# Two queues for the first load, and an earlier place for the first ordinary pair's q and k, in a linear-attention and feed-forward kernel

## The chip, the cores and the metric

The kernel runs on one core of one Trainium2 chip. The metric is the device time of one execution in microseconds (us), less is better; a time of several runs is their median. The engines are TensorE (PE, matmuls; its weight loads are a row of their own, PEld), VectorE (DVE), ScalarE (ACT), GpSimd (POOL) and SyncE (SP). They run side by side and wait for each other by semaphores. SP, ACT and POOL each issue DMA transfers into a queue of their own; 16 DMA engines move the data of all queues.

## The reference

Two layers, one after the other. The first is linear attention with decay over blocks of 64 tokens, for 4 batches, 8 heads, 768 tokens and a head size of 64:

```python
for b in range(nb):                                   # nb = 768 / 64 = 12
    sl = slice(b * block, (b + 1) * block)
    qb, kb, vb = q[:, :, sl], k[:, :, sl], v[:, :, sl]
    intra = np.einsum('bhic,bhjc->bhij', qb, kb) * Dmask[None]      # lam^(i-j), j <= i
    intra = np.einsum('bhij,bhjd->bhid', intra, vb)
    inter = np.einsum('bhid,bhde->bhie', qb * lam_pow[None], kv_state)
    out[:, :, sl] = intra + inter
    kb_dec = kb * rev_pow[None]
    kv_state = lam_block[None, :, None, None] * kv_state + np.einsum('bhsd,bhse->bhde', kb_dec, vb)
```

The second is a gated feed-forward layer on the 3072 tokens, with a model size of 512 and a hidden size of 2048:

```python
x = attn_out.transpose(0, 2, 1, 3).reshape(3072, 512)
h = x @ w_in                                          # 512 x 2048
g = h * np.cos(h)
out = g @ w_out                                       # 2048 x 512
```

All inputs and the output are float32; the kernel multiplies in bfloat16 and sums in float32.

## The kernel before

**Tiling.** Tokens are cut into 24 groups of 128. The feed-forward layer takes them in tiles of 4, 2, 2, 2, 2, 2, 2, 4 and 4 groups (`TILES`). For a tile, 16 hidden slices are made (`hidden`, L732, into `ps_h`), ACT takes the cosine (L738), DVE multiplies (L744, into `g`), and the second product (`project`, L778, into `ps_f`) sums the 16 slices in four steps of four, each step with one quarter of w_out. ACT copies the sum out (L792) and SP stores it.

**Attention.** The first four groups are two *spans*: the first 256 tokens of batch 0 and of batch 1, two neighbouring tokens in a partition. A span's q, k and v come in one load each (`add_span_load`, L259, issued at L253). DVE or POOL scales q and k by powers of lam (`prep`, L593), TensorE transposes them (L601, `ps_t`), ACT copies the transposes out (L604), then follow scores (L612), masking on DVE (L617), values (L638), the carried state (L625, L644) and the copies into `xT` (L652), which the first feed-forward tile reads. All other groups go in *ordinary pairs*, group n of two batches. Their loads are `add_load` (L275); a pair's q is scaled on DVE and POOL (L329), its k converted on ACT or POOL (L333), its v scaled (L337). The first ordinary pair consists of groups 4 and 5. Its q and k are transposed on TensorE (L359) and copied by DVE (L362); later pairs are transposed by DMA (L365).

**Order.** No scheduler of the compiler decides the order. The kernel lists all work as tasks with an engine, a planned duration, dependencies and a priority; `Planner.order` simulates the engines with these numbers and writes the instructions in the order of planned start. `SETUP` holds the times at which the planner takes each engine, and the DMA engines, to be free at first. Its numbers are not the chip's; they only set the order. Each engine then runs its own instructions strictly in that order, so a waiting instruction holds everything behind it on its engine.

**Loads.** The string `ORDER` names the early loads in order: q0, k0, q1, k1, v0, v1 are the spans'; i0 to i5 the six parts of w_in (of 2, 2, 1, 3, 4, 4 hidden slices); o0 to o3 the quarters of w_out; q4, q5, k4, k5 the first ordinary pair's; v4 and v5 follow. The spans' q and k and all ordinary loads are issued by SP, the spans' v and all weights by POOL, which converts float32 to bfloat16 on the way. `start` (L252) can make an issue wait for another load to have landed: v0 waits for q0 (the argument `kept[0:1]`); q4 waits for a gate product of the first feed-forward tile (`pace`, L755, three slices before its last); o3 waits for q4; v4 waits for k4. In the program before, POOL issues v0, v1, i0, i1, prepares k of span 1, issues i2, i3, i4, i5, o0, o1, o2, then o3. SP issues q0, k0, q1, k1 of the spans, then q4, q5, k4, k5, v4, v5. When TensorE has made the first tile's 16 slices, it runs seven steps of `ps_f` (with o0, o1 and o2), the eight transposes of q of the first ordinary pair, two more steps, the transposes of k, and so on.

**The very first microseconds.** ACT loads lam (L188) and an activation table (L189); TensorE spreads lam over all partitions (`ps_lam`, L875) between filler matmuls that keep it busy (`keep_awake`, L861, `ps_idle`); ACT and DVE make the scales from it (L877 to L891), ACT loads the table of the sine (L893).

Of the kernel before, what the change touches and what calls it, by code (L numbers as in the profile page):

```python
# [10 lines left out]
F32 = mybir.dt.float32  # L11
# [7 lines left out]
SPANS = 2  # L19
# [15 lines left out]
STATE_OUT = [("ACT", "ACT"), ("ACT", "ACT")]  # L35
ORDER = "q0 k0 q1 k1 v0 v1 i0 i1 i2 i3 i4 i5 o0 o1 o2 q4 q5 k4 k5 o3"

# [19 lines left out]
class Planner:  # L57
# [3 lines left out]

    SETUP = {"POOL": 3.7, "DVE": 4.4, "ACT": 6.0, "SP": 0.85, "DMA": 1.95}

# [81 lines left out]
def kernel(  # L145
# [41 lines left out]
    lam_row = consts.tile([1, H], F32)  # L187
    nc.scalar.dma_start(out=lam_row, in_=lam.unsqueeze(0))  # L188
    nc.scalar.preload_act_table_set("natural_log_exp_and_others")  # L189
    ones = consts.tile([1, P], F32)  # L190
# [40 lines left out]
    halves = [slice(i * D, (i + 1) * D) for i in range(2)]  # L231
    live = {}

# [24 lines left out]

    def add_span_load(name, src, x, prio, deps):  # L259
        def emit(_):  # L260
            if on_pool:
                t = span_v[x]
            else:
                if ("raw", x) not in live:
                    live["raw", x] = work.tile([P, 2, H, 2, D], F32, tag="g", name="sp_f")
                t = live[name, "sp", x] = live["raw", x][:, "qk".index(name[0])]
            return start(nc.gpsimd if on_pool else nc.sync, t.rearrange("u h s d -> u h (s d)"),
                         src[x, :, 0:2 * P, :].rearrange("h (u s) d -> u h (s d)", s=2), deps)

        on_pool = name == "v_f"  # L270
        issue, load_t[name, "sp", x] = dma("POOL" if on_pool else "SP", 1.5, 1.0 if on_pool else 0.5, emit, prio, deps,
                                           lat=0.95 if on_pool else 1.0)
        return load_t[name, "sp", x]

    def add_load(n, name, src, prio, deps=()):  # L275
        b, c = where(n)

        def emit(_):
            t = loads.tile([P, H, D], F32, tag=name, name=name)
            live[name, n] = t  # L280
            i = start(nc.sync, t, src[b, :, c * P:(c + 1) * P, :].transpose([1, 0, 2]), deps)
            if (name, n) == ("q_f", 2 * SPANS):

                tc.add_manual_dep(i.ins, pace[0].ins.ins.name, mybir.DependencyInfo(
                    mybir.DependencyClass.Sync, mybir.DependencyReason.DATA), reason="order of loads")
            return i

        issue_t[name, n], load_t[name, n] = dma("SP", LOAD_US, 0.85, emit, prio, deps, get=name,
                                                lat=1.9 if name == "v_f" and n < 2 * SPANS + 2 else 1.0)
        return load_t[name, n]  # L290
# [3 lines left out]
    def add_w(which, c, prio, deps=()):  # L294
        def emit(_):
            if which == "in":
# [7 lines left out]
        _, w_t[which, c] = dma("POOL", 2.68 * part, 0.8, emit, -2000.0 if early else prio, deps,  # L304
                               lat=1.2)
        return w_t[which, c]
# [272 lines left out]
    def add_span(x):  # L579
# [75 lines left out]
        s_first = None  # L655
        so, kt, v_t = [[], []], [], [load_t["v_f", "sp", x]]
        for hp in range(2):
            eq, ek = QK[x]["q"][hp], QK[x]["k"][hp]
            a = pl.add(eq, us[eq], [load_t["q_f", "sp", x]], partial(prep, name="q", hp=hp, e=eq), pa(-0.9 + 0.1 * hp))
            kt.append(pl.add(ek, us[ek], [load_t["k_f", "sp", x]], partial(prep, name="k", hp=hp, e=ek), pa(-0.9 + 0.1 * hp)))  # L660
            if x:
# [50 lines left out]

    h_last, o_last = {}, {}
    hid, closing = [], None

    def add_ffn(i):
# [4 lines left out]
        for f in range(KF):  # L721
            gate[f] = []
            blocks = [(0, 2), (2, 4)] if i == 0 and f < SPLIT else [(0, nb)]
            for b0, b1 in blocks:
# [27 lines left out]
                a.frees = [d]  # L752
                gate[f].append(d)
                if i == 0 and f == KF - 3:
                    pace.append(d)  # L755
# [61 lines left out]
    for at, name in enumerate(names):  # L817
# [3 lines left out]
        if name == f"q{2 * SPANS}":  # L821
            deps = []
        if name == f"v{2 * SPANS}":
            deps = [load_t["k_f", 2 * SPANS]]
        if name == "o3":
            deps = [load_t["q_f", 2 * SPANS]]
# [13 lines left out]
    add_span_state(first_scores, prio_attn(2 * SPANS, 0.2))  # L840
    pr = SPANS
    for i in range(len(TILES)):
        while 2 * pr < first[i + 1]:
            if pr + 1 in ALONE:
                add_scores(pr + 1, prio_attn(2 * pr + 2, 0.2))
# [26 lines left out]

    keep_awake(1.2, 1.6)
    lam_ps = bank((idle.bank[0] + 4) % BANKS, [P, H], F32, "ps_lam")
# [18 lines left out]
    nc.scalar.activation(warm, halfpi, AF.Sin)  # L893
    now = 2.8
    for t in plan:
        if t.eng == "PE" and t.start < lead_end.start + 1e-6:
            keep_awake((t.start - now) * 0.95 if now < 3.0 else t.start - now, now)
            now = t.end
        if t.emit:
            t.ins = t.emit(t)  # L900
# [30 lines left out]
```

## Time and profile before

| what | us |
|---|---|
| median of 3 runs | 203.09 (202.97 to 203.18) |
| the profiled execution, whole | 202.54 |
| its span on the core | 200.8 |
| TensorE busy in it | 195.9 |
| `ps_h` L732, 596 matmuls, and `ps_f` L778, 400 matmuls, busy | 91.1 and 91.4 |
| DVE, ACT, POOL busy | 116.3, 119.4, 64.9 |
| bytes moved by DMA | 33.93 MB, 169 GB/s on average |

The profile is one execution, taken by the hardware profiler. All times in it are microseconds from the span's start. A line of the timeline has the start, the duration, the engine, the source line, the operation, output and inputs, and in brackets the engine's idle time before it and what ended that. Lines with a q behind an engine's name (SPq, ACTq) are DMA issues; their duration is that of the issue, not of the transfer. The chain of waits goes back from the last instruction, at each step to what released it, and is shown in order of time with start and duration. In lists of DMA queues, q1 is SP's queue, q10 ACT's and q0 POOL's, and the numbers are packets, MB and the time that packets took as a share of the 16 engines' time.

### The profile page before, as it was taken

How to read it: one execution, taken by the hardware profiler on the slowest of the kernel's cores; microseconds unless marked ns; L12 is line 12 of the kernel's file. 1: busy time of each engine (PE TensorE's matmuls, PEld its weight loads, DVE VectorE, ACT ScalarE, POOL GpSimd, SP SyncE). 2: the span in 40 equal slices, each digit the busy share in tenths (PEclk: the TensorE clock that was granted, in tenths of full speed). 3: DMA queues.
4: the chain of work that ended last, by engine and by line, in shares of the span. 5: the costliest groups of instructions: out<-in, count | busy, mean ns of one | idle time of the engine just before them, and what ended most of it. 6: DMA issues, size and time to landing. Idle time of an engine off the chain costs nothing.

```text
span 200.8 us, 5951 instructions
## 1 busy us (share of the span) xinstructions
PE 195.9 (98%) x2473; PEld 116.8 (58%) x2473; DVE 116.3 (58%) x230; ACT 119.4 (59%) x241; POOL 64.9 (32%) x85
## 2 busy tenths in 40 slices
PE   6999999999999999999999999999999999999994
PEld 3477444558757757766658676755445544444452
DVE  3978771269756948758458575835588354444001
ACT  4878771149658768666639666644887564345120
POOL 5893003085235360635555353545500000000000
PEclk9999999999999999999999999999999999999999
DMA  5999999999889997999999899979910010111112
GB/s 163 303 190 204 203 199 216 209 238 225 200 197 225 262 202 177 239 179 253 189 275 245 188 207 194 277 141 261 243 23 3 3 52 0 52 55 52 52 52 104
DMA packets 96620, 33.93 MB, mean 169 GB/s; under 512 B 84690, under 2 KB 93650, under 8 KB 96594
## 3 DMA queue, kind: packets, MB, share of 16 engines
q1 hardware_dynamic: 89088, 28.78, 63.2%
q0 software_dynamic: 7360, 4.72, 16.4%
q8 instruction: 19, 0.31, 0.7%
q10 hardware_dynamic: 146, 0.07, 0.1%
q14 instruction: 7, 0.06, 0.1%
HBM read 27.26 MB, written 6.29 MB: 167 GB/s over the span
## 4 chain that ended last, share of the span: by engine, by line
PE 95%; DMA 2%; ACT 0%; DVE 0%; SPq 0%; issue 0%; ACTq 0%; DVEq 0%
PE ps_h L732 42%; PE ps_f L778 42%; DMA sp_f<-in_k_dram 2%; PE ps_s L407 2%; PE ps_o L502 2%; PE ps_o L470 2%; PE ps_kv L419 1%; PE ps_t L601 1%; PE ps_s L612 1%; PE ps_o L638 1%; PE ps_kv L625 1%; PE ps_x L470 0%; PE ps_idle L870 0%; PE ps_t L359 0%; DVE k_sp L593 0%; PE ps_o L644 0%
## 5 line engine op out<-in xcount | busy, mean ns | idle before, releaser
L744 DVE TENSOR_TENSOR g<-ps_h,cos 128x256 bf16<-128x256 f32 (+1 forms) x149 | 73.1, 501 | 42.0 <-ACT cos L738 41.1
L738 ACT ACTIVATE cos<-ps_h,halfpi 128x256 f32<-128x256 f32 (+1 forms) x149 | 75.9, 536 | 29.3 <-PE ps_h L732 28.2
L778 PE MATMUL ps_f<-w_out_sb,g 128*128 128x512 bf16 (+2 forms) x400 | 91.4, 371 | 0.0
L732 PE MATMUL ps_h<-xT,w_in_sb 128*128 128x256 bf16 (+1 forms) x596 | 91.1, 303 | 0.0
L732 PEld LDWEIGHTS <-w_in_sb 128*128 128x128 bf16 x596 | 57.5, 98 | 30.1 <-DVE xT L510 0.4
L778 PEld LDWEIGHTS <-g 128*128 128x128 bf16 x400 | 37.6, 98 | 37.2
L329 POOL TENSOR_TENSOR qk<-q_f,q_scale 128x512 bf16<-128x512 f32 x19 | 20.0, 1067 | 34.7 <-DMA q_f<-in_q_dram 17.6
L792 ACT COPY o_sb<-ps_f 128x512 f32<-128x512 f32 (+1 forms) x24 | 13.7, 572 | 24.7 <-PE ps_f L778 24.5
L337 POOL TENSOR_TENSOR v_s<-v_f,v_scale 128x512 bf16<-128x512 f32 x19 | 19.6, 1042 | 9.8 <-DMA v_f<-in_v_dram 5.2
L412 DVE TENSOR_TENSOR s_m<-ps_s,mask 128x512 bf16<-128x512 f32 x20 | 13.0, 685 | 4.2 <-PE ps_s L407 3.6
L333 POOL CAST qk<-k_f 128x512 bf16<-128x512 f32 x18 | 11.0, 611 | 10.4 <-DMA k_f<-in_k_dram 10.2
L510 ACT CAST xT<-ps_o 128x512 bf16<-128x512 f32 x11 | 6.0, 588 | 9.0 <-PE ps_o L502 5.6
L425 DVE TENSOR_TENSOR sum<-sum,ps_kv 128x512 f32<-128x512 f32 x15 | 10.2, 682 | 0.6
L430 ACT CAST S<-sum 128x512 bf16<-128x512 f32 x15 | 9.1, 616 | 0.9 <-DVE sum L425 0.8
L253 POOL DMA_DIRECT2D w_out_sb<-in_moe_w_out_dram x4 | 3.0, 784 | 15.8 <-DMA q_f<-in_q_dram 15.8
L792 DVE COPY o_sb<-ps_f 128x384 f32<-128x384 f32 x1 | 0.6, 557 | 11.6 <-DMA out_dram<-o_sb 11.6
L470 PEld LDWEIGHTS <-v_s 64*64 64x64 bf16 x320 | 4.0, 107 | 4.2 <-issue 3.4
L870 PE MATMUL ps_idle<-blank 128*128 128x512 f32 (+2 forms) x8 | 4.7, 707 | 1.7 <-DVE blank L215 1.7
L487 DVE COPY spare<-ps_o 1x1 f32<-1x1 f32 x6 | 0.9, 156 | 8.4 <-PE ps_o L470 8.4
L617 DVE TENSOR_TENSOR s_m_sp<-ps_s,mask_sp 128x512 bf16<-128x512 f32 x8 | 5.1, 684 | 1.2 <-PE ps_s L612 1.2
L470 PE MATMUL ps_o<-s_m,v_s 64*64 64x64 bf16 x256 | 5.2, 196 | 0.0
L502 PE MATMUL ps_o<-qkT,S 64*64 64x64 bf16 x304 | 4.9, 195 | 0.0
(76 smaller groups left out, 90.1 us busy)
## 6 DMA issues: line engine op xcount, KB each, us to landing
q_f<-in_q_dram SPq DMA_DIRECT2D x20, 256.0 KB, 3.9
k_f<-in_k_dram SPq DMA_DIRECT2D x20, 256.0 KB, 4.2
v_f<-in_v_dram SPq DMA_DIRECT2D x20, 256.0 KB, 5.1
out_dram<-o_sb SPq DMA_DIRECT2D x19, 256.0 KB, 2.5
w_out_sb<-in_moe_w_out_dram POOLq DMA_DIRECT2D x4, 512.0 KB, 12.4
sp_f<-in_q_dram SPq DMA_DIRECT2D x2, 512.0 KB, 4.9
sp_f<-in_k_dram SPq DMA_DIRECT2D x2, 512.0 KB, 5.5
w_in_sb<-in_moe_w_in_dram POOLq DMA_DIRECT2D x2, 512.0 KB, 8.9
```

Source lines behind the costliest of these rows:

```text
L329: vec[e].tensor_mul(new_qk()[:, 0, :, s], live.pop(("q_f", 2 * pr + s)), q_scale[:, c, :].unsqueeze(2).to_broadcast([P, H, D]))
L333: (nc.scalar.copy if early else nc.gpsimd.tensor_copy)(new_qk()[:, 1, :, s], live.pop(("k_f", 2 * pr + s)))
L337: vec[e].tensor_mul(live["v_s", 2 * pr + s], live.pop(("v_f", 2 * pr + s)), v_scale[:, c, :].unsqueeze(2).to_broadcast([P, H, D]))
L412: nc.vector.tensor_mul(t, live["s", pr][s], mask.unsqueeze(1).to_broadcast([P, H, D]))
L425: nc.vector.tensor_add(new, live["sum", pr, 0] if half else live["sum", pr - 1, 1], live["kv", pr][half])
L430: nc.scalar.copy(new_S(pr, half), live["sum", pr, half])
L470: yield lambda h=h: nc.tensor.matmul(o[halves[h % 2], h // 2], lhsT=live["v_s", n0 + s][m, h, :], rhs=live["s_m", n0 + s][m, h, :], start= ...
L732: nc.tensor.matmul(t[:, :n], lhsT=w_in_sb[:, kd, f * P:(f + 1) * P], rhs=live["xT", i][:, kd, at], start=(kd == 0), stop=(kd == KD - 1))
L738: nc.scalar.activation(c[:, :n], live["h", i, f, at.start][:, :n], AF.Sin, bias=halfpi)
L744: return nc.vector.tensor_mul(live["g", i][:, f, at], live.pop(("h", i, f, at.start))[:, :n], live.pop(("c", i, f, at.start))[:, :n])
L778: nc.tensor.matmul(live["f", i, j, piece][:, :width], lhsT=live["g", i][:, f, j * P:(j + 1) * P], rhs=w_out_sb[:, f, part], start=(f == 0) ...
L792: (nc.scalar.copy if eng == "ACT" else nc.vector.tensor_copy)(o[:, :width], live["f", i, j, piece][:, :width])
```

## The change

The first span's q is loaded in two halves by heads: SP loads heads 0 to 3; ACT, right behind its load of lam, loads heads 4 to 7. The first scaling of q then waits for SP's half, the second for ACT's. The wait of v0, which was for the whole of q0, is now for ACT's half.

In `ORDER`, q4, q5, k4 and k5 move from behind o2 to behind o0. q4 waits for i4 to land in place of the gate product, o1 waits for q4 (before, o3 did), and v4 waits for o1 (before, for k4). The program that results differs in its order: POOL issues o1 and o2 behind q4's landing, prepares q5, and issues o3 then. TensorE runs one step of `ps_f` behind the first tile's slices, the transposes of q, two steps, the transposes of k, two steps (the second is the first that needs o1), the state and scores, then seven steps with o1 and o2; before it these were seven, two, two, and later one at a time. DVE's scaling of q4 stands four gate products earlier than the first tile's last, ACT's conversion of k4 in front of the last cosine. The numbers of the planner (`SETUP`, load durations and latencies) change, and one more dependency ties the lone scores of pair 3 to the last gate product of a tile, so that later stages also stand in a somewhat different order. The filler in front of `ps_lam` has 128 columns in place of 320, and one of 512 bfloat16 columns becomes 128 of float32.

```diff
-ORDER = "q0 k0 q1 k1 v0 v1 i0 i1 i2 i3 i4 i5 o0 o1 o2 q4 q5 k4 k5 o3"
+ORDER = "q0 k0 q1 k1 v0 v1 i0 i1 i2 i3 i4 i5 o0 q4 q5 k4 k5 o1 o2 o3"
...
-    SETUP = {"POOL": 3.7, "DVE": 4.4, "ACT": 6.0, "SP": 0.85, "DMA": 1.95}
+    SETUP = {"POOL": 3.7, "DVE": 3.9, "ACT": 5.5, "SP": 0.85, "DMA": 1.5}
...
     nc.scalar.dma_start(out=lam_row, in_=lam.unsqueeze(0))
+    raw_0 = work.tile([P, 2, H, 2, D], F32, tag="g", name="sp_f")
+    late_q = nc.scalar.dma_start(out=raw_0[:, 0, H // 2:].rearrange("u h s d -> u h (s d)"),
+                                 in_=q[0, H // 2:, 0:2 * P, :].rearrange("h (u s) d -> u h (s d)", s=2))
...
     def add_span_load(name, src, x, prio, deps):
+        on_pool = name == "v_f"
+        first_q = (name, x) == ("q_f", 0)
+        cut = slice(0, H // 2) if first_q else slice(0, H)
...
-            return start(nc.gpsimd if on_pool else nc.sync, t.rearrange("u h s d -> u h (s d)"),
-                         src[x, :, 0:2 * P, :].rearrange("h (u s) d -> u h (s d)", s=2), deps)
...
+            return start(nc.gpsimd if on_pool else nc.sync, t[:, cut].rearrange("u h s d -> u h (s d)"),
+                         src[x, cut, 0:2 * P, :].rearrange("h (u s) d -> u h (s d)", s=2), deps)
+
+        part = dma("POOL" if on_pool else "SP", 0.75 if first_q else 1.5, 1.0 if on_pool else 0.5, emit, prio, deps,
+                   lat=0.95 if on_pool else 1.0)[1]
+        load_t[name, "sp", x] = [part, part]
+        if first_q:
+            issue = pl.add("SP", 0.0, [part.issue], None, prio)
+            issue.ins = late_q
+            late = pl.add("DMA", 0.75, [issue], None, prio, lat=1.0)
+            late.issue = issue
+            load_t[name, "sp", x] = [part, late]
+        return load_t[name, "sp", x][1]
...
-            if (name, n) == ("q_f", 2 * SPANS):
-
-                tc.add_manual_dep(i.ins, pace[0].ins.ins.name, mybir.DependencyInfo(
-                    mybir.DependencyClass.Sync, mybir.DependencyReason.DATA), reason="order of loads")
...
-        issue_t[name, n], load_t[name, n] = dma("SP", LOAD_US, 0.85, emit, prio, deps, get=name,
-                                                lat=1.9 if name == "v_f" and n < 2 * SPANS + 2 else 1.0)
+        issue_t[name, n], load_t[name, n] = dma("SP", 0.95 if n < 2 * SPANS + 2 else LOAD_US, 0.85, emit, prio, deps, get=name,
+                                                lat=1.6 if name == "v_f" and n < 2 * SPANS + 2 else 1.0)
...
         if name == f"q{2 * SPANS}":
-            deps = []
+            deps = [w_t["in", 4]]
         if name == f"v{2 * SPANS}":
-            deps = [load_t["k_f", 2 * SPANS]]
-        if name == "o3":
+            deps = [w_t["out", 1]]
+        if name == "o1":
             deps = [load_t["q_f", 2 * SPANS]]
...
         add_ffn(i)
+        if i and pr in alone and pr in (3,):
+            alone[pr].deps.append(gates[i])
...
-    issue_t["q_f", 2 * SPANS].deps += pace
...
-    keep_awake(1.2, 1.6)
+    keep_awake(0.6, 1.6)
...
-    now = 2.8
+    now = 2.3
```

More of the change, by code (lines that the diff above doesn't have):

```diff
@@ L231 @@
     halves = [slice(i * D, (i + 1) * D) for i in range(2)]
-    live = {}
+    live = {("raw", 0): raw_0}
     unit = [MM(n * P, 4 * KF) + MM(DM, KF * n) + ATT * n for n in TILES]
@@ L266, in emit @@
                 t = live[name, "sp", x] = live["raw", x][:, "qk".index(name[0])]
-            return start(nc.gpsimd if on_pool else nc.sync, t.rearrange("u h s d -> u h (s d)"),
-                         src[x, :, 0:2 * P, :].rearrange("h (u s) d -> u h (s d)", s=2), deps)
[L270 to L273, printed above, removed]
+            return start(nc.gpsimd if on_pool else nc.sync, t[:, cut].rearrange("u h s d -> u h (s d)"),
[10 more added lines that the diff above has]
+        return load_t[name, "sp", x][1]
     def add_load(n, name, src, prio, deps=()):
@@ L304, in add_w @@
         _, w_t[which, c] = dma("POOL", 2.68 * part, 0.8, emit, -2000.0 if early else prio, deps,
-                               lat=1.2)
+                               lat=2.0 if which == "out" and c else 1.2)
         return w_t[which, c]
@@ L655, in add_span @@
         s_first = None
-        so, kt, v_t = [[], []], [], [load_t["v_f", "sp", x]]
+        so, kt, v_t = [[], []], [], [load_t["v_f", "sp", x][0]]
         for hp in range(2):
             eq, ek = QK[x]["q"][hp], QK[x]["k"][hp]
-            a = pl.add(eq, us[eq], [load_t["q_f", "sp", x]], partial(prep, name="q", hp=hp, e=eq), pa(-0.9 + 0.1 * hp))
-            kt.append(pl.add(ek, us[ek], [load_t["k_f", "sp", x]], partial(prep, name="k", hp=hp, e=ek), pa(-0.9 + 0.1 * hp)))
+            a = pl.add(eq, us[eq], [load_t["q_f", "sp", x][hp]], partial(prep, name="q", hp=hp, e=eq), pa(-0.9 + 0.1 * hp))
+            kt.append(pl.add(ek, us[ek], [load_t["k_f", "sp", x][hp]], partial(prep, name="k", hp=hp, e=ek), pa(-0.9 + 0.1 * hp)))
             if x:
@@ L711, in add_span_state @@
         u.bank_frees = [[x]]
-    h_last, o_last = {}, {}
+    h_last, o_last, gates = {}, {}, {}
     hid, closing = [], None
@@ L753, in add_ffn @@
                 gate[f].append(d)
+                if f == KF - 1:
+                    gates[i] = d
                 if i == 0 and f == KF - 3:
@@ L841 @@
     pr = SPANS
+    alone = {}
     for i in range(len(TILES)):
@@ L844 @@
             if pr + 1 in ALONE:
-                add_scores(pr + 1, prio_attn(2 * pr + 2, 0.2))
+                alone[pr + 1] = add_scores(pr + 1, prio_attn(2 * pr + 2, 0.2))[0]
             add_stretch(pr, first_update if pr == SPANS else None)
@@ L893 @@
     nc.scalar.activation(warm, halfpi, AF.Sin)
-    now = 2.8
+    now = 2.3
     for t in plan:
         if t.eng == "PE" and t.start < lead_end.start + 1e-6:
-            keep_awake((t.start - now) * 0.95 if now < 3.0 else t.start - now, now)
+            keep_awake((t.start - now) * 0.95 if now < 2.5 else t.start - now, now)
             now = t.end
```

## The prediction

> **What bounds the kernel now.** I read the shares first, then the chain of waits in order of time, then the timeline around each place where the chain is not TensorE, then the DMA packets there in short windows.
>
> ```profile
> PE 195.9 (98%) x2473; PEld 116.8 (58%) x2473; DVE 116.3 (58%) x230; ACT 119.4 (59%) x241; POOL 64.9 (32%) x85
> ```
>
> TensorE is busy for 195.9 of 200.8 us, so a gain must come from starting its real work sooner, or from a wait inside it. The chain shows where there is one:
>
> ```profile
> 1.32 4.92 DMA sp_f<-in_k_dram
> ...
> 9.63 0.91 PE ps_idle L870 x2
> 10.55 0.02 issue
> 10.57 0.40 PE ps_t L601 x4
> 10.97 0.55 PE ps_kv L625 x8
> ...
> 16.31 12.68 PE ps_h L732 x72
> 28.99 6.04 PE ps_f L778 x28
> 35.03 0.45 PE ps_t L359 x8
> ```
>
> The chain opens with the first k span load (landed at 1.32 + 4.92 = 6.24). At 9.63 TensorE runs filler (`ps_idle`) for 0.91 us. From 10.57 one real group follows the next: the 28 matmuls from 28.99 take 6.04 us, 0.216 each, which is also the rate at the end (80 pieces in 13.87 us). There is no wait to remove after 17 us; only the head can give time, and everything else can only lose it. What holds the head:
>
> ```profile
> 5.05 1.96 POOL L253 DMA_DIRECT2D v_sp<-in_v_dram  x2 [1.39 <-DMA sp_f<-in_q_dram]
> ...
> 9.47 2.04 POOL L593 TENSOR_TENSOR k_sp<-sp_f,k_sp 128x512 bf16<-128x512 f32 x2 [0.96 <-DMA sp_f<-in_k_dram]
> ...
> 10.56 0.23 PEld L601 LDWEIGHTS <-k_sp 128*128 128x128 bf16 x4 [0.85 <-POOL k_sp L593]
> ...
> 16.69 0.33 PEld L732 LDWEIGHTS <-w_in_sb 128*128 128x128 bf16 x4 [0.23 <-DMA w_in_sb<-in_moe_w_in_dram]
> ```
>
> The second span's k landed at 3.28 + 6.0 = 9.28; POOL prepared it, TensorE waited 0.85 us for POOL. POOL's own queue (v of both spans, then w_in) opens when the first q has landed (0.81 + 3.9 = 4.71; POOL issues at 5.05); v of span 0 lands 5.7 us later, at 10.75, 0.15 before the `ps_kv` that reads it starts (10.90), and w_in's third part, i2, makes TensorE wait at 16.69. So two DMA streams, SP's and POOL's, set the head, each with 0.2 us or less to spare. The packets of SP's queue in 2.0:2.5, 2.5:3.0 and 3.3:3.8, and of ACT's queue in 199.2:199.3 (packets, MB, share):
>
> ```profile
> q1 hardware_dynamic: 132, 0.07, 56.5%
> q1 hardware_dynamic: 115, 0.06, 59.4%
> q1 hardware_dynamic: 338, 0.17, 114.1%
> q10 hardware_dynamic: 48, 0.02, 79.5%
> ```
>
> The stream starts at about 1.9 and gives for a microsecond only 247 packets where it later gives 676. The ACT store at the end, issued at 198.30, sends 48 packets in 0.1 us only 0.9 us later: a queue need not start so slowly.
>
> **The change: q's first span in halves.** Removed: 512 of SP's first 1024 packets. Added: one ACT issue behind lam's (0.80 + 0.54 = 1.34). The first k still stands behind 1 MB of q and k in all, so a full stream would bring it no sooner. What can help is the slow start. By the end store's row ACT's packets flow from about 1.40 + 0.85 = 2.25. Missing packets from there: half of 338 - 132 (103), then 338 - 115 (223), then 35 in 3.0:3.2 (100 where 135 would fit): 361, at 676 per us 0.53 us. That is the upper bound. The lower is 0: the start may be slow for a reason that both queues share. I take 0.45, by the end store as the nearest row, less 0.08 for its own first packets. [...]
>
> The first k then lands at 5.8, the second at 8.8, and POOL's k preparation starts at 9.0 instead of 9.47 (POOL's issues before it end at 8.51 now). POOL's stream must move too: v now waits for q's late half. The halves share the engines with k; if each queue gets its turn, both halves are in when the whole q would be or up to 0.2 later, 4.3 to 4.5 with the gain, so v is issued 0.2 to 0.45 earlier. As both streams keep the engines full until long after 17 us, the end of i2 follows the bytes in front of it, and moves by the 0.45 also.
>
> What is hidden: the ACT issue delays the table load (1.37) by about 0.55, the issue before it being 0.54; it ends at 3.2 instead of 2.65. The logarithm that follows ran at 3.65, behind `ps_lam`, whose filler shrinks from 320 to 128 columns (1.43 us for both passes; 0.4 of that is 0.57). So the scale is ready at 4.0 to 4.4 (now 4.36), as q's first half lands. Behind ACT's issue stand that load, five small activations and qT's copies; the covers are the q load and DVE's q preparations, which end at 6.14 now, and without them a late scale would cost its delay, at most 0.55, on the first k alone, where the filler of 0.91 takes it up.
>
> **The change: q4, q5, k4, k5 behind w_out's first quarter.** SP's queue issues them when i4 has landed (13.05 + 8.0 = 21.0), not at 28.74. Then o1 and o2 wait on POOL for q4, and the preparation of q5, then o3, is queued behind them; v4 waits for o1. TensorE runs one group of o0, the transposes of q, two groups, the transposes of k, one group, and only then o1. The matmuls are the same 64 up to the next `ps_h` (28+8+8+12+4+4 against 4+8+8+28+8+8), so TensorE's own cost is nothing; what counts is when data come.
>
> The packets of 35.5:37.5, and POOL's timeline:
>
> ```profile
> q0 software_dynamic: 374, 0.38, 118.9%
> ```
>
> ```profile
> 32.55 0.74 POOL L253 DMA_DIRECT2D w_out_sb<-in_moe_w_out_dram  x1 [15.83 <-DMA q_f<-in_q_dram]
> 33.31 1.06 POOL L329 TENSOR_TENSOR qk<-q_f,q_scale 128x512 bf16<-128x512 f32 x1
> ```
>
> In that window only packets of o3 (POOL's queue) moved, none of v4, though SP had issued v4 at 33.89 (it took 6.4 us to land). So I let q4 wait until o0 is through. o0 lands at 14.45 + 11.5 = 25.95; 256 KB take 1.0 us (550 packets of 256 B in 30.7:31.2, of 1024), so q4 lands at 27.0. [...]
>
> On the old clock (all of it 0.45 sooner): POOL issues o1 and o2 (0.8 each) by 28.6, prepares q5 (1.06) by 29.65; the transposes stand at 28.99 + 0.86 = 29.85. Spare: 0.2. o1 is needed at 29.85 + 0.45 + 1.73 + 0.45 + 0.86 = 33.35. It lands at 27.0 + 6.6 = 33.6 by o3's row, or at 27.0 + 2.6 (o3's issue to its flow) + 2.6 (spacing of o0, o1, o2) + 0.5 = 32.7 from an idle ring. I take the middle, 33.15: no wait, and keep 0 to 0.3 for the range. o2, 2.6 later, is needed at 33.35 + 0.86 + 1.00 + 0.86 = 36.07, with as little to spare. k's copies on ACT, v4 and v5 have 0.5 us or more. DVE's preparation of q4 (0.69) pushes four gate products, which win 0.17 each back against TensorE's 0.865 a group. Later stages get their loads no later, so I cost them nothing; the cover is that no TensorE wait stands there now, and if one came it would cost its length.
>
> **Sum.** Profiled execution: span 200.8, 1.74 around it, 202.54 in all; less 0.45 is 202.09. That execution lies 0.55 under the median shown, 203.09; there it is 202.64, so 202.6.
>
> **Rivals.**
> 1. *The slow start is not the queue's.* Gain 0, and the late half lands up to 0.2 later, v with it: v of span 0 had 0.15, so 0 to 0.1 lost: 203.1 to 203.2. For it: packets came in irregular bursts at first (12 to 31 per 0.1 us). Against it: the end store's start.
> 2. *The head gains, o1 takes it back.* 0.45 won, 0.3 to 0.5 lost at 33.35 or 36.07: 202.8 to 203.1. For it: o3's 6.6 us. Against: o3 was issued while two loads stood before it.
> 3. *The late half holds POOL's queue* (slower). If ACT's half is served only after SP's first k, as v4 was behind o3, q's second half lands with it at about 6.2, and v is issued 1.5 us later. SP's stream ends at about 8.95, POOL's flow (8.45 now, v's 5.05 + 3.4) starts at 9.95: an engine gap of 1.0 us, in which v, i0, i1 and i2 all move, less v's 0.15: +0.9, time 204.0. It decides from 0.3 us of delay on. For it: the window 35.5:37.5. Against: two hardware queues may well alternate where a software queue does not.
> 4. *The loads come too late for the new place of the transposes* (slower): past 27.2, each 0.1 of q4's landing is lost at 29.85. By the slowest row (a q load issued at 34.93, 7.2 us) q4 lands at 28.2: 1.0 lost, less the gain of 0.45: 203.6. For it: v4's and that load's rows. Against: they were issued as o3 began, not as o0 ended.
>
> **How the numbers follow.** Chances: forecast 0.45, rival 1 0.17, rival 2 0.14, rival 3 0.14, rival 4 0.10. Under 0.2% (0.41 us) a measurement cannot be told from no change. Faster: the forecast, 0.45; slower: rivals 3 and 4 and the far edge of 1 and 2 (0.03), 0.27; the same: the rest of 1 and 2, 0.28. Range: the lower end is the full 0.53 and i2's wait (0.23) both won, with 0.1 of scatter: 202.2; the upper end reaches past rival 4 towards 3: 203.9. The forecast's own range is 202.2 to 202.7.
>
> **What would show it.** Right: more than 200 packets in each half us between 2.25 and 3.25 on both queues together; the first k at or under 5.9, `ps_t` of the second k at 10.1; v issued before 5.05; `ps_h` from about 15.85; no TensorE gap at the first transposes of q (L368) or the fifth `ps_f` group. Wrong: v's issue after 5.3, a gap in front of `ps_kv`, or weight loads of `ps_f` or `ps_t` that end a wait for w_out, POOL or DMA.

## The result, and the profile after

The changed kernel takes 206.38 us (median of 6 runs, 204.80 to 207.65) against 202.92 for the kernel before: a ratio of 1.0151, 95% interval 1.0113 to 1.0189. That is 3.1 us slower (0.0151 of 202.9; the two medians lie 3.5 apart); the forecast was 202.6, and the time lies above the whole range, 202.2 to 203.9. An execution over 1.5% longer than the fastest of its kernel, of which e8, e10, e12, e13 and e16 below have one each, counts in the medians and not in the ratios. The runs now spread by 2.9 us where the kernel before spreads by less than 0.5. The profiled execution, 207.21 with a span of 205.5, is one of the long ones.

The page of the changed kernel, the shares by engine and the chain of waits by engine:

```profile
PE 195.0 (95%) x2448; PEld 118.7 (58%) x2474; DVE 115.6 (56%) x230; ACT 119.1 (58%) x241; POOL 64.7 (31%) x85
...
PE 64%; DMA 24%; SPq 5%; POOL 2%; issue 2%; DVE 1%; ACT 1%; ACTq 0%; POOLq 0%
```

TensorE's busy time is what it was (195.9, and some of its records are missing here). What is new is that 24% of the chain is DMA (2% before). Its opening in order of time (start, duration, what):

```profile
1.37 5.14 DMA sp_f<-in_q_dram
...
10.34 2.04 POOL k_sp L602 x2
12.38 1.48 POOL w_in_sb L256 x2
13.86 7.88 DMA w_in_sb<-in_moe_w_in_dram
21.74 0.02 issue
21.76 7.08 DMA q_f<-in_q_dram
...
29.38 5.70 DMA w_out_sb<-in_moe_w_out_dram
...
35.50 8.59 DMA v_f<-in_v_dram
```

One load hangs on the other: ACT's half of q (issued 1.37, landed 6.51) holds POOL, POOL's i4 releases q4, q4's landing releases o1, and o1's landing releases v4 and v5. These are five transfers of 5 to 9 us in one line; the chain of the kernel before has one, of 4.92. Where TensorE waits (total, times, longest):

```profile
...
PE ps_t L610 <- DVE q_sp L602: 1.0, 1, 1.0
PE ps_o L479 <- DVE v_s L346: 0.9, 1, 0.9
PE ps_t L368 <- POOL qk L338: 0.5, 1, 0.5
PE ps_s L416 <- DMA qkT<-qk: 0.5, 1, 0.5
PE ps_f L789 <- DMA w_out_sb<-in_moe_w_out_dram: 0.2, 1, 0.2
...
```

The first is in the head, the third and fifth are at the new place of q's transposes and at o2, the second is at 44.92 for v5, and the fourth at 117.15 for a transpose by DMA, in a stage that neither named part of the change touches. First `ps_h` 14.14 before, 15.86 now (+1.7); the second tile's first `ps_h` 45.92, now 49.53 (+3.6); last matmul 197.70, now 201.95 (+4.25).

The head on DVE and POOL (timeline):

```profile
3.88 0.69 DVE L602 TENSOR_TENSOR q_sp<-sp_f,q_sp 128x512 bf16<-128x512 f32 x1
6.54 0.69 DVE L602 TENSOR_TENSOR q_sp<-sp_f,q_sp 128x512 bf16<-128x512 f32 x1 [1.97 <-DMA sp_f<-in_q_dram]
6.81 1.96 POOL L256 DMA_DIRECT2D v_sp<-in_v_dram  x2 [3.11 <-DMA sp_f<-in_q_dram]
8.76 1.51 POOL L256 DMA_DIRECT2D w_in_sb<-in_moe_w_in_dram  x2
10.34 2.04 POOL L602 TENSOR_TENSOR k_sp<-sp_f,k_sp 128x512 bf16<-128x512 f32 x2
```

SP's half is there at 3.73, a microsecond sooner than the whole load was; ACT's half lands behind the first k (6.35). So v goes out at 6.81, not 5.05, and POOL's preparation of k waits for POOL's own issues instead of k.

### The profile page after: what moved, and what is told of

Its sections match the earlier page's. It is cut to its first block, busy times and chain, and to the rows that moved or that the text cites. A ratio compares the mean times of both kernels' runs of the same rounds, so it can differ in the third digit from the quotient of the medians.

```text
span 205.5 us, 5928 instructions
## 1 busy us (share of the span) xinstructions
PE 195.0 (95%) x2448; PEld 118.7 (58%) x2474; DVE 115.6 (56%) x230; ACT 119.1 (58%) x241; POOL 64.7 (31%) x85
## 4 chain that ended last, share of the span: by engine, by line
PE 64%; DMA 24%; SPq 5%; POOL 2%; issue 2%; DVE 1%; ACT 1%; ACTq 0%; POOLq 0%
PE ps_f L789 29%; PE ps_h L741 29%; DMA v_f<-in_v_dram 9%; DMA w_in_sb<-in_moe_w_in_dram 4%; SPq L256 4%; DMA q_f<-in_q_dram 3%; DMA w_out_sb<-in_moe_w_out_dram 3%; DMA sp_f<-in_q_dram 3%; DMA qkT<-qk 2%; PE ps_o L511 1%; PE ps_o L479 1%; PE ps_s L416 1%; PE ps_kv L428 1%; POOL k_sp L602 1%; SPq L812 1%
## 5 line engine op out<-in xcount | busy, mean ns | idle before, releaser
L789 PE MATMUL ps_f<-w_out_sb,g 128*128 128x512 bf16 (+2 forms) x378 | 88.6, 370 | 2.2 <-issue 1.3
L741 PEld LDWEIGHTS <-w_in_sb 128*128 128x128 bf16 x596 | 57.6, 98 | 29.8
L883 PE MATMUL ps_idle<-blank 128*128 128x128 f32 (+1 forms) x10 | 5.1, 632 | 1.7 <-DVE blank L218 1.7
L530 DVE TENSOR_TENSOR xT<-ps_o,cross 128x256 bf16<-128x256 f32 x8 | 3.0, 420 | 4.0 <-ACT cross L536 2.1
```

The lines of the kernel that those rows point to most:

```text
L741: nc.tensor.matmul(t[:, :n], lhsT=w_in_sb[:, kd, f * P:(f + 1) * P], rhs=live["xT", i][:, kd, at], start=(kd == 0), stop=(kd == KD - 1))
L789: nc.tensor.matmul(live["f", i, j, piece][:, :width], lhsT=live["g", i][:, f, j * P:(j + 1) * P], rhs=w_out_sb[:, f, part], start=(f == 0) ...
```

## The experiments

The changed kernel and seventeen experiments. Times are medians; a ratio is to the kernel before, measured beside it on the same chip, and a cost "in us" is the ratio less 1, times 202.9.

| run | what it is | median (runs) | ratio, 95% interval |
|---|---|---|---|
| | the changed kernel | 206.38 (6) | 1.0151, 1.0113 to 1.0189 |
| e1 | changed, first q whole on SP | 205.70 (4) | 1.0119, 1.0069 to 1.0168 |
| e2 | before, split alone | 203.99 (8) | 1.0056, 1.0037 to 1.0075 |
| e3 | changed, v released by SP's half | 205.27 (4) | 1.0125, 1.0098 to 1.0153 |
| e4 | changed, both halves on SP | 206.79 (4) | 1.0206, 1.0169 to 1.0244 |
| e5 | e1, q4 on i3 | 205.48 (4) | 1.0114, 1.0055 to 1.0173 |
| e6 | e1, v4 on k4 | 204.99 (10) | 1.0091, 1.0056 to 1.0125 |
| e7 | old early order, new later order | 205.07 (10) | 1.0086, 1.0050 to 1.0122 |
| e8 | before, v released by the first k | 204.10 (10) | 1.0045, 1.0018 to 1.0072 |
| e9 | early move alone | 203.32 (7) | 1.0029, 1.0016 to 1.0042 |
| e10, e15 | changed, old later order | 203.82 (4), 204.10 (10) | 1.0042, 1.0026 to 1.0059; 1.0043, 1.0015 to 1.0072 |
| e11 | before, new fillers (and one v_s earlier on POOL) | 202.67 (10) | 1.0001, 0.9985 to 1.0017 |
| e12 | e2, v released by SP's half | 203.28 (10) | 1.0023, 1.0005 to 1.0041 |
| e13 | e7, load planned at 1.05 | 203.27 (10) | 1.0014, 0.9993 to 1.0035 |
| e14 | e7, load planned at 1.12 | 203.75 (10) | 1.0044, 1.0017 to 1.0070 |
| e16 | e7, v5's scaling behind the masks | 204.28 (8) | 1.0060, 1.0033 to 1.0088 |
| e17 | e11, v5's scaling before the masks | 203.67 (10) | 1.0044, 1.0024 to 1.0063 |

### The head: whose half is late, and what that holds

e1 undoes the split in the changed kernel; e2 makes it alone in the kernel before, by the lines of the change, with v0's wait on ACT's half. e1:

```diff
-    late_q = nc.scalar.dma_start(out=raw_0[:, 0, H // 2:].rearrange("u h s d -> u h (s d)"),
-                                 in_=q[0, H // 2:, 0:2 * P, :].rearrange("h (u s) d -> u h (s d)", s=2))
...
-        cut = slice(0, H // 2) if first_q else slice(0, H)
+        cut = slice(0, H)
```

> The changed kernel with the first part undone: SP loads the whole first q again, ACT only lam; every engine's order, the fillers and the early place of q4 to k5 stay as in the changed kernel. Theory A (the two parts lose separately: ACT's half is served only after SP's first k and costs the head 1.7 us, the early place of q4 costs the rest): v is issued at 5.0 to 5.2 again, the first slice of ps_h starts at 14.0 to 14.4, and the time is 206.4 less 1.7, 204.7 (204.2 to 205.2). Rival B (the TensorE waits at the early transposes exist only because the streams run late): those waits go too, time 202.7 to 203.3. Rival C (the new fillers and the new order cost the head, not the split): ps_h still starts after 15.2, time above 205.7.

> The kernel before with the first part alone: SP loads heads 0 to 3 of the first q, ACT heads 4 to 7 behind lam, and v of span 0 waits for ACT's half; order, fillers and later loads as before. Theory A: ACT's half lands at 6.3 to 6.6, v is issued at 6.6 to 6.9, ps_h starts 1.5 to 1.9 later than 14.14, and the time is 202.9 plus 1.7, 204.6 (204.2 to 205.0). Rival C (half of the head's loss is the shorter filler ahead of ps_lam, which left TensorE at half speed from 5.2 on): with the longer filler kept, ps_t of the first q runs at 0.40, and the loss is 0.8 to 1.0: 203.7 to 204.0.

e1: v is issued at 5.11 and `ps_h` starts at 14.53, the head is nearly back, but 2.4 us of loss stay: A's head holds, its size for the rest does not, and B and C fall. e2 costs 1.1 us. In its profiled execution (203.31, the shortest) ACT's half landed at 5.08, v was issued at 5.38 and `ps_h` started 0.46 late. So the late half is not late by a fixed amount: 5.08 here, 5.03 in e12, 6.09 in e3, 6.12 in e15, 6.51 in the changed kernel. e2's time is in rival C's range, but C's sign is missing: with the longer filler kept, the first `ps_t` of q still took 0.63. The filler costs nothing by e11 (0.0, within 0.3).

e3 and e12 release v by SP's half (in the changed kernel and in e2); e8 prices POOL's held queue alone, with no split at all. e8's edit:

```diff
-                         src[x, :, 0:2 * P, :].rearrange("h (u s) d -> u h (s d)", s=2), deps)
+                         src[x, :, 0:2 * P, :].rearrange("h (u s) d -> u h (s d)", s=2), [load_t["k_f", "sp", 0]] if deps else [])
```

e3's and e12's:

```diff
-                         src[x, cut, 0:2 * P, :].rearrange("h (u s) d -> u h (s d)", s=2), deps)
+                         src[x, cut, 0:2 * P, :].rearrange("h (u s) d -> u h (s d)", s=2), [load_t["q_f", "sp", 0][0]] if deps else [])
...
-                tc.add_manual_dep(i.ins, late_q.ins.name, mybir.DependencyInfo(
+                tc.add_manual_dep(i.ins, load_t["q_f", "sp", 0].issue.ins.ins.name, mybir.DependencyInfo(
```

> The changed kernel, but v of span 0 waits for SP's half of q (landed 3.73) and not for ACT's (6.51); nothing else differs. If POOL's held queue is what costs the head (rival 3 of the prediction), v is issued at 4.1 to 4.3, w_in's parts all move up by 1.5 or more, and 0.8 to 1.7 of the 3.5 come back: 204.7 to 205.6. If it is the late second half on DVE and the half-speed TensorE behind it, the head stays at 15.5 or later: 206.0 to 206.6. The first k may land later, since v's packets now run beside it.

> The kernel before with one wait changed: v of span 0 is released by the landing of SP's first k (6.24) in place of the first q (4.75); no split, the same fillers, the same order. It prices by itself POOL's held queue, rival 3 of the prediction (v, i0, i1, i2 all 1.5 us later less 0.15 and the gap that SP's stream leaves): v is issued at 6.5 to 6.7 and the time is 202.9 plus 0.9, 203.8 (203.5 to 204.1). If DMA has no idle time to lose there, 202.9 to 203.2; if the whole 1.5 reaches TensorE, 204.3 or more.

> The kernel before with the split, and v of span 0 released by SP's half (landed 3.8) and not by ACT's. If POOL's held queue is all that the split costs (1.1 alone), 202.7 to 203.2, and the head starts as before or sooner. If the late second half on DVE and TensorE, or v's packets beside the first k, cost too, 203.5 to 204.3. Only if the split's own gain (TensorE's lam path 0.5 sooner, full DMA rate 0.3 sooner) gets through, under 202.5.

POOL in e8, the issue that was moved:

```profile
6.62 1.96 POOL L253 DMA_DIRECT2D v_sp<-in_v_dram  x2 [2.96 <-DMA sp_f<-in_k_dram]
```

e8: 0.9 us (0.4 to 1.5), `ps_h` at 15.02: the price that rival 3 gave, 0.9. e12: 0.5 (0.1 to 0.8), in the profiled execution `ps_h` at 14.34. So by these medians 0.6 of the split's 1.1 is POOL's held queue; the intervals leave room for much less and for nearly all of it. e3's median lies in the range of its first expectation, but by the ratios only 0.5 of the 3.1 come back, and the intervals overlap: its head is at 14.31, but i1 landed at 16.62 (i0 at 13.71) and TensorE waited 1.3 us for it. Why i1 took so long stays open. v issued earlier does not bring w_in sooner than the kernel before has it: in e12 v goes out at 4.07 (5.05 before), and i0, i1 and i2 land at 13.61, 14.98 and 16.75 (13.52, 14.94 and 16.65 before).

e4 puts both halves on SP:

```diff
+            issue = pl.add("SP", 0.0, [part.issue], lambda _: nc.sync.dma_start(
+                out=raw_0[:, 0, H // 2:].rearrange("u h s d -> u h (s d)"), in_=q[0, H // 2:, 0:2 * P, :].rearrange("h (u s) d -> u h (s d)", s=2)), prio)
```

> The changed kernel with both halves of the first q issued by SP, one behind the other, none by ACT. If the loss is that ACT's queue gets no turn beside SP's, the second half lands at 4.6 to 5.0, v is issued at 4.9 to 5.3, and the time is that of the whole load, 204.7 (204.2 to 205.2). If the loss comes with loads of 256 KB instead of 512 KB, or with one more wait on DVE, the second half lands at 5.5 or later and the time stays above 205.7.

The halves landed at 3.65 and 4.39, sooner than expected, and v was issued at 4.70; yet the first k landed at 7.67 and the time is 206.8. The first expectation had the landing and not the time, the second the time and not the landing: the stream had its slow phase twice, in 2.2 to 2.6 (64 packets) and again as the first k began, in 4.2 to 4.6 (67 packets where e1 has 275). What starts the second one stays open.

What the first microsecond looks like, DMA packets by queue (q1 is SP's, q10 ACT's): in 2.6 to 3.0, before and e4,

```profile
q1 hardware_dynamic: 93, 0.05, 61.0%
```

```profile
q1 hardware_dynamic: 264, 0.13, 110.7%
```

and with the split, e2 in 3.4 to 3.8 and the changed kernel in 4.2 to 5.2:

```profile
q10 hardware_dynamic: 216, 0.11, 91.5%
q1 hardware_dynamic: 22, 0.01, 8.2%
```

```profile
q1 hardware_dynamic: 354, 0.18, 59.6%
q10 hardware_dynamic: 288, 0.15, 48.6%
```

The full rate does come 0.4 us sooner with a load of half the size, but with SP's queue alone: e4 has no ACT half, and in the changed kernel 2.75 to 3.25 has 333 packets, all of SP's. ACT's first packets come at 3.1 (e2) or 4.0 (changed), 1.8 and 2.6 us after the issue. In the changed kernel the queues then share what one would have had (642 packets in that microsecond; SP's alone moved at 676 per us before). e2's 216 to 22 is no sharing: SP's queue had moved 515 packets by 3.4, its whole half of q, and the 22 are the slow first ones of k. In neither does k gain: the first k landed at 6.24 before, 6.28 in e2, 6.35 in the changed kernel.

### The early move

e9 is the early move alone: whole q, and one planner number put back, so that all later stages stand in the old order on every engine, but for two pairs of neighbouring issues on SP (LOAD_US is 1.22):

```diff
-        issue_t[name, n], load_t[name, n] = dma("SP", 0.95 if n < 2 * SPANS + 2 else LOAD_US, 0.85, emit, prio, deps, get=name,
+        issue_t[name, n], load_t[name, n] = dma("SP", LOAD_US, 0.85, emit, prio, deps, get=name,
```

> The changed kernel with the whole first q on SP and one planner number put back (the load of q4 to v5 planned at 1.22 and not at 0.95): q4 to k5 still stand behind o0, but the later stages fall back to the order of the kernel before, on every engine. It prices the early move alone. If the parts add up (whole-q kernel 2.5 over before, the later order alone 1.9 of it), 0.6 to 1.0 is left: 203.7 to 204.2. If the waits at the transposes of q, for o1 and for v4 (0.84, 0.73, 0.24 in the whole-q profile) each cost their length, 204.6 to 205.0. If the later order is harmless once it is not tight, 205.3 or more, as with the whole q.

0.6 us (0.3 to 0.8), at the low edge of the first expectation; the median, 203.32, is below its range. In its profile q4 landed at 27.22 and o1 at 33.62, and the wait at the new place is small:

```profile
PE ps_t L368 <- POOL qk L338: 0.3, 1, 0.3
```

What POOL does between q4's landing and that wait, from the chain of e9:

```profile
27.24 0.02 POOLq L256
27.26 0.49 issue
27.75 0.45 POOL w_out_sb L256
...
29.24 1.08 POOL qk L338
```

e5 and e6 ask what sets the loads there. e5 releases q4 by i3, e6 releases v4 by k4, both in e1:

```diff
-            i = start(nc.sync, t, src[b, :, c * P:(c + 1) * P, :].transpose([1, 0, 2]), deps)
+            i = start(nc.sync, t, src[b, :, c * P:(c + 1) * P, :].transpose([1, 0, 2]), [w_t["in", 3]] if (name, n) == ("q_f", 4) else deps)
...
+            i = start(nc.sync, t, src[b, :, c * P:(c + 1) * P, :].transpose([1, 0, 2]), [load_t["k_f", 4]] if (name, n) == ("v_f", 4) else deps)
```

> The changed kernel with the whole first q on SP (205.7), and q4 released by i3's landing (18.7) in place of i4's (21.3): issued 2.6 us earlier, everything else the same. Theory S (SP's queue gets no turn while POOL's queue still has packets of i5 and o0): q4 moves no data sooner, lands with o0 at 27.0 to 27.9 as before, TensorE waits at the transposes of q as long, time 205.4 to 206.0. Theory T (a load just takes 6.4 us from its issue): q4 lands at 25.1, o1 is issued at 25.6 and lands at 32.4, the waits at the transposes (0.84) and for o1 (0.73) go, time 204.0 to 204.4.

> The changed kernel with the whole first q on SP (205.7), and v4 released by k4's landing, as in the kernel before, in place of o1's. DMA stood nearly idle in 30.0 to 31.0 (46 packets), so v4 and v5 should flow there: they land before 32, TensorE's wait ahead of ps_o at 43 goes (0.25 in this profile, 1.0 in the changed kernel's). Theory A (each wait costs its own length, none hides another): 204.9 to 205.5. Rival (v4 and v5 take 2 us of the queue from o1, which is waited for at 34.2): o1 lands later than 35.5, time 206 or more.

The chain of waits of e5:

```profile
18.49 9.07 DMA q_f<-in_q_dram
```

and of e6:

```profile
29.66 12.82 DMA v_f<-in_v_dram
```

In time e5 is theory S: issued 2.9 us sooner than in e1, q4 took 9.07 instead of 6.42 and landed at 27.56, beside o0 (27.33). Theory S's mechanism is not what the packets show. e5 in 18.5 to 22.0:

```profile
q0 software_dynamic: 712, 0.71, 122.7%
```

e5 in 22.5 to 25.0, then e6 in 34.0 to 39.0:

```profile
q0 software_dynamic: 377, 0.38, 90.2%
q1 hardware_dynamic: 381, 0.10, 29.5%
```

```profile
q0 software_dynamic: 761, 0.76, 90.9%
q1 hardware_dynamic: 756, 0.19, 29.0%
```

SP's queue is served while POOL's holds packets of i5 and o0. For 3.6 us after q4's issue nothing of it moves; then both queues move the same number of packets, and as SP's are of 256 B and POOL's of 1 KB, SP's loads get a fifth of the bytes (0.10 of 0.48 MB, and 0.19 of 0.95). Why q4 then lands only as o0 does is not shown.

e6's time lies in theory A's range, but without its signs: v4, issued at 29.25, had its first packets at 33.4, when POOL's queue flowed again; v5 landed at 42.5, when o1, o2 and o3 were through; o1 was not delayed (34.14); TensorE still waited 0.4 for v5. Released 5.9 us sooner than in e1, v5 landed 0.2 sooner. So v4's wait for o1's landing is not what makes v4 late; that POOL's queue is follows from these times and was not tried alone.

### The later order

e7 is e1 with the old early order; e11 is e7, and e10 and e15 are the changed kernel, with the one line of e9 put back:

```diff
-ORDER = "q0 k0 q1 k1 v0 v1 i0 i1 i2 i3 i4 i5 o0 q4 q5 k4 k5 o1 o2 o3"
+ORDER = "q0 k0 q1 k1 v0 v1 i0 i1 i2 i3 i4 i5 o0 o1 o2 q4 q5 k4 k5 o3"
...
-            deps = [w_t["in", 4]]
+            deps = []
...
-            deps = [w_t["out", 1]]
+            deps = [load_t["k_f", 2 * SPANS]]
-        if name == "o1":
+        if name == "o3":
...
+    issue_t["q_f", 2 * SPANS].deps += pace
```

> The changed kernel with both parts undone by hand: the whole first q on SP, the early order of the kernel before (o1, o2 ahead of q4, q4 on the gate product, o3 on q4, v4 on k4), but the changed planner numbers, so that the later stages (SP's queue of loads, transposes and stores above all) stand in the changed kernel's order and not in the old one's. If the later order costs nothing, as the prediction said, this is the kernel before: 202.7 to 203.1. If TensorE's waits for DMA transposes at 79.8 (1.2 us in the last run of the whole load) and at 117 (0.6 in the changed kernel) come from the later order itself, 203.5 to 204.3.

> The changed kernel, split and early move as they are, with the same one planner number put back, so that the later stages stand in the old order. If the later order is a part of the loss by itself, this is 1.0 to 2.0 under the changed kernel's 206.4: 204.4 to 205.4. If the later waits only follow from the late head and the late loads, nothing changes: 206.0 to 206.8.

> The kernel before with nothing of the change left but the two shorter fillers on TensorE ahead of the first span's work and one v_s on POOL two places earlier. If the fillers are harmless, 202.8 to 203.2; if they leave TensorE at half speed in the head (ps_t at 0.64 in place of 0.40, as in the changed kernel), 203.5 or more. The difference from the run with the old early order and the new later order (205.1) is then the later order's alone.

> The changed kernel with the one planner number put back, once more, for a usable profile (three of the four runs before gave 203.5 to 204.0). Expected 203.5 to 204.0; TensorE without a wait behind the second tile, a wait of about 0.5 ahead of the transposes of q, and the head's delay of 0.3 to 1.7 by when ACT's half lands. If the later waits return, over 205.

e7 has neither named part: whole q, the old ORDER string, the old releases. It has only the new planner numbers and the fillers, and costs 1.7 us (1.0 to 2.5), more than either expectation. e10 and e15 are the other half: both parts as changed, the one number of e9 put back; 2.2 us come back, also more than expected. (e15 is e10 once more and gives the profile.) e11, e7 with the number back, costs nothing. So this number, 0.95 for 1.22 as the planned duration of q4 to v5, is the largest part of the loss.

What it does is visible in the program. Six loads planned 0.27 shorter let the planner place all that reads them earlier. Before each pair's scores TensorE has this many feed-forward matmuls of 512 columns (two of 256 count as one), from pair 4 on:

```
old later order (before, e9, e11): 222 268 312 364 414 460 504 560
changed kernel, e1:                216 260 308 360 404 452 500 548
e7:                                214 260 304 356 404 452 496 548
```

4 to 12 fewer, 0.9 to 2.6 us at 0.216 each; and in the changed kernel and e1 the values of the first ordinary pair, which read v4 and v5, stand behind 48 `ps_f` matmuls instead of 56 (in e7 behind 56). TensorE's own work is the same and only its order differs, so each place is now nearer to its data. TensorE's waits in e7, and in e1:

```profile
...
PE ps_o L483 <- DVE s_m L425: 0.6, 1, 0.6
PE ps_s L420 <- DMA qkT<-qk: 0.6, 1, 0.6
...
```

```profile
...
PE ps_s L416 <- DMA qkT<-qk: 1.2, 1, 1.2
PE ps_t L368 <- POOL qk L338: 0.7, 1, 0.7
PE ps_f L789 <- DMA w_out_sb<-in_moe_w_out_dram: 0.6, 1, 0.6
...
```

From the second tile's first `ps_h` to the last matmul every profile with the old later order (but e10's) takes 151.8 to 151.9 us; e7 takes 152.5, e1 153.0, e5 153.3, e6 152.5, the changed kernel 152.4, and e3 and e4 151.8 as well. e1, e3, e4, e5, e6 and the changed kernel have the same instructions in the same order there, so the same order can meet these waits or miss them. That this is the spread of the changed kernel's times is likely and not shown, as each kernel has one profile.

Is it a matter of degree or one swap? e13 and e14 plan the load in e7 at 1.05 and 1.12; e16 and e17 move one DVE instruction (e17's edit is below, e16 inserts behind the last mask).

> The kernel with the old early order (205.1 with the load of q4 to v5 planned at 0.95, 202.7 with 1.22), now planned at 1.05. In TensorE's order the scores of the ordinary pairs then stand behind 218, 262, 308, 360, 406, 454, 500, 552 feed-forward matmuls: 4 to 8 earlier than with 1.22 (222, 268, 312, 364, 414, 460, 504, 560), 0 to 4 later than with 0.95. Theory P (scores placed earlier than the DMA transposes, k and v allow make TensorE wait, more the earlier they stand): 203.2 to 204.6. Theory Q (one particular swap at 0.95 does it, as the two v_s that change places on DVE or a store between two transposes on SP): 202.6 to 203.0, or 205 as with 0.95.

> The same with the load planned at 1.12: the scores stand behind 220, 264, 310, 364, 412, 456, 500, 552 matmuls, 0 to 8 earlier than with 1.22. Theory P: between the run with 1.05 and 202.7, so 202.8 to 203.8. Theory Q: the same as one of the ends.

> The old early order with the new later order (205.1, load planned at 0.95), and one DVE instruction moved: the scaling of v5 goes back behind the two score masks of the first ordinary pair, where it stands in the kernel before. In the profile of 0.95 DVE waited 3.23 us for v5 with both masks queued behind it, and ps_o came 0.6 to 0.75 late. Theory Q (this swap, and separate waits later): the wait ahead of ps_o at 43 goes and 0.5 to 0.8 come back, 204.2 to 204.7. If the swap is the whole loss of the later order, 202.6 to 203.2. If another engine makes ps_o wait as long, 205 again.

> The counterpart: the order that costs nothing (202.7, load planned at 1.22) with only that DVE instruction moved ahead of the two masks. Theory Q: DVE waits for v5 at 41 to 42, ps_o comes 0.5 to 0.8 late, 203.2 to 203.6. If the masks had time to spare there, 202.6 to 202.9; if the whole loss is this swap, 204.5 or more.

By the medians it is not degree alone: 1.05 costs 0.3 us (-0.1 to 0.7), and 1.12, nearer to the old order, 0.9 (0.3 to 1.4); the intervals overlap, so these two do not rule degree out. In both, DVE's scaling of v5 stands between the two score masks: with 1.05 v5 landed at 41.73 and `ps_o` did not wait, with 1.12 at 42.09 and `ps_o` waited 0.45. (Each also waits once for a gate product, 0.6 and 0.4.) In e7 it stands in front of both masks. DVE in e7:

```profile
41.98 0.81 DVE L350 TENSOR_TENSOR v_s<-v_f,v_scale 128x512 bf16<-128x512 f32 x1 [3.23 <-DMA v_f<-in_v_dram]
42.71 1.27 DVE L425 TENSOR_TENSOR s_m<-ps_s,mask 128x512 bf16<-128x512 f32 x2
```

The scores that the masks read started at 40.31, and in e11 the first mask starts 0.6 after them; here both stand some 1.8 us behind an instruction that waits for v5. e17, the good order with only that instruction moved:

```diff
     plan = pl.order()
+    first_v, masks = d_t[2 * SPANS + 1], [So[2 * SPANS], So[2 * SPANS + 1]]
+    at = [t is first_v for t in plan].index(True)
+    plan.pop(at)
+    plan.insert(min(i for i, t in enumerate(plan) if any(t is m for m in masks)), first_v)
```

costs 0.9 us (0.5 to 1.3), a little over theory Q's range, and e16, the swap taken out of e7, still costs 1.2 (0.7 to 1.8). Behind the head, TensorE's waits for another engine or a load in e16's profile are for transposes alone:

```profile
PE ps_s L420 <- DMA qkT<-qk: 1.3, 3, 0.6
```

So in e7 the 1.7 is one swap on DVE and a few waits for transposes (0.9 and 1.2 one by one, within the intervals). In the changed kernel itself the masks stand in front of v5's scaling, so the swap is not its loss; there v4 and v5 are late behind o1 to o3 (0.9 at 44.92), o1 is read ahead of the state and the scores and not behind them as in e9 (1.0 us of TensorE's work), and the transposes are waited for. How the 2.2 us divide among these three was not tried one by one. Of the 2.2 us between the profiles of the changed kernel and e15, 1.2 stand in the head, where both have the same instructions (see the last section). The profiles of e1 and e9 show the later order without that: their heads differ by 0.1, and e9 is 1.25 us shorter from the first `ps_h` to the second tile's first and 1.22 from there to the last matmul.

## Why the prediction was wrong

**The step that failed most** is the last of the early move: "Later stages get their loads no later, so I cost them nothing; the cover is that no TensorE wait stands there now, and if one came it would cost its length." The loads were indeed no later for that reason (v5 landed at 41.96 in e7 and at 41.92 in e17, which has the old order); their readers stood earlier. The cover belonged to the old order, and the new one has it no more. The term measured 1.7 us alone (e7) and 2.2 in the changed kernel (its 3.1 less the 0.9 of e10 and e15).

**The head: "I take 0.45, by the end store as the nearest row."** Wrong in sign. The store's 0.9 us from issue to flow did not carry over; ACT's load took 1.8 to 2.6. The bound of 0 was right for the first k. Another issuer brought no bandwidth (642 packets per us on both queues in 4.2 to 5.2 of the changed kernel, 676 on SP's alone before). A gain of 0 would still have been too kind, as the split costs 1.1 alone; 0.6 of it come back when v no longer waits for the slower queue (e12).

**Rival 3** is what happened to the head, at a chance of 0.14. Its price of 0.9 is what e8 measures (0.4 to 1.5). Two of its sentences did not hold as written: the half is not always served behind the first k (5.03 to 6.51), and once both queues flow they do share, 354 to 288 packets in 4.2 to 5.2 of the changed kernel. In the profiled execution the head lost 1.7, not 0.9; TensorE's rate has a part in that, see the last section.

**The early move, "TensorE's own cost is nothing; what counts is when data come":** right in kind, and the sizes were good on the old clock: q4 predicted at 27.0, measured 27.22 in e9; o1 33.15, measured 33.62. For q4 that is a right number from a wrong picture: the prediction let q4 wait until o0 is through, and e5 shows both queues moving (in e9 o0 landed at 26.46, 25.97 before). The move costs 0.6, for the spare 0.2 at the transposes was used up: the sum put POOL's issues right behind q4's landing, and in e9 0.5 us lie between, as between q4's landing (32.02) and o3's issue (32.55) in the kernel before, so that q5 was ready at 30.32 and not at 29.65, and TensorE waited 0.3. In the changed kernel, with the head late, q4 landed at 28.84 and o1 at 35.07. **"k's copies on ACT, v4 and v5 have 0.5 us or more"** failed for v5: it landed at 44.09 and TensorE waited 0.9. The window 35.5 to 37.5, shown in the prediction, held the reason (v4, issued at 33.89, moved nothing while POOL's queue flowed there), and I used it for q4 and not for v4.

**Rival 4** came true beside rival 3, since a late head makes i4 late and that makes q4 late. I had taken the rivals as alternatives. The three parts one by one, 0.6 (e9) + 1.1 (e2) + 1.7 (e7), are 3.4, and the change measured 3.1 (2.3 to 3.8). That is no proof that costs add: the split and the early move together cost 0.9 (e10, e15), not 0.6 + 1.1, so one seems to hide a part of the other.

**What was right:** the table load ended at 3.12 (3.2 predicted), the scale was ready at 3.84 (4.0 to 4.4), DVE's first half started at 3.88, and the fillers cost nothing. The signs that were to show an error did: v issued at 6.81 (5.3 was the limit), and weight loads of `ps_t` and `ps_f` that end waits for POOL and w_out. Only 143 packets moved in 2.25 to 2.75 where 200 were asked.

No run beats the kernel before: e11 and e13 equal it, and none brings the first k or the first three parts of w_in more than 0.2 us sooner.

## What to carry to other kernels

A constant that only feeds a planner is a change to every order that it computes: compare the whole program, and for each instruction that reads a load count the work in front of it, before costing a stage at nothing. A load split over two queues is as late as its slower half for whoever waits for both (here 6.51 against 3.73); give no other queue's release to it. When a rival's delay feeds the next rival's condition, both can come true at once: price the pair, which can cost less than the sum (the split and the early move here: 0.9 against 0.6 + 1.1).

## What the hardware showed that was not expected

A transfer's time from issue to landing can be mostly queueing: q4, whose 1024 packets would take 0.9 us at the rate of 30.7 to 31.2 in the kernel before (an estimate from 550 in 0.5), took 6.42 us issued at 21.36 and 9.07 issued at 18.49, and in e6 v5, issued at 29.66 ahead of o1's full flow, 12.82. The first packets of SP's first load beside POOL's flow came 3.2 us after the issue in e1 (q4, 24.5), 3.5 in the changed kernel (q4, 25.2), 3.6 in e5 (q4, 22.0) and 4.1 in e6 (v4, 33.4), but 1.0 for q4 in the kernel before (29.8). What sets this time stays open.

TensorE ran the head at half its rate for longer in the changed kernel than in e15, which has the same instructions there: a group of four transposes kept it for 0.43 us (8.22 to the next start at 8.65), in e15 for 0.22 (7.59 to 7.81). Matmuls of the changed kernel, then of e15:

```profile
7.29 0.61 PE L610 MATMUL ps_t<-ident,q_sp 128*128 128x128 bf16 x4 [1.03 <-DVE q_sp L602]
8.22 0.64 PE L610 MATMUL ps_t<-ident,k_sp 128*128 128x128 bf16 x4
9.64 0.64 PE L621 MATMUL ps_s<-qT_sp,kT_sp 64*64 64x128 bf16 x16
11.15 0.40 PE L610 MATMUL ps_t<-ident,q_sp 128*128 128x128 bf16 x4
```

```profile
6.89 0.58 PE L610 MATMUL ps_t<-ident,q_sp 128*128 128x128 bf16 x4 [0.64 <-DVE q_sp L602]
7.59 0.39 PE L610 MATMUL ps_t<-ident,k_sp 128*128 128x128 bf16 x4
8.65 0.42 PE L621 MATMUL ps_s<-qT_sp,kT_sp 64*64 64x128 bf16 x16 [0.16 <-ACT kT_sp L613]
```

After a wait of 1.03 us the same group takes 0.64 until about 11; after one of 0.64 it is at 0.39 from 7.59 on. `ps_h` starts at 15.86 in the one and at 14.63 in the other. The mean granted clock of the profile reads 1.00 in both and does not show it, but the record of the clock in the trace opens at full speed only at 10.89 in the changed kernel and at 7.32 in e15 (5.37 in the kernel before). That the longer wait did this is not shown: e16 and e13 have the same instructions in the head and no wait there over 0.25, and full speed is recorded from 9.45 in e16 and from 6.40 in e13. One group in e16, then in e13:

```profile
7.33 0.63 PE L614 MATMUL ps_t<-ident,k_sp 128*128 128x128 bf16 x4
```

```profile
7.12 0.40 PE L614 MATMUL ps_t<-ident,k_sp 128*128 128x128 bf16 x4
```

What decides when TensorE goes to full speed is not shown; no run here varied the wait alone.
